# Keys as eight token classes, paired taps in four blocks, gate factors as value columns, and a new written-out order, in a two-layer kernel

## The chip, the cores and the metric

The kernel runs on one core of a Trainium2 chip. The metric is device time in microseconds of one execution. Three runs of the kernel before are at hand, and a profile of one execution, taken by the hardware profiler.

## The reference, cut to what matters

Two layers are computed and written side by side. Layer A is a short filter on the keys, a product with the values, and a convolution over the whole sequence. Layer B is attention in four segments with a memory that is carried from one to the next. S = 2048 tokens, D = 640 channels, H = 32 heads of 20, N = 4 segments of L = 512.

```
def A(q, k, v, shift_k, ssm_k, ssm_D):
    k_shift[t] = sum over j < 4 of k[t - j] * shift_k[:, j]
    kv = k_shift * v
    y = irfft(rfft(kv, 2S) * rfft(ssm_k, 2S))[:S] + kv * ssm_D
    return q * y

def B(x, wq, wk, wv, wo, beta):
    phi = lambda t: where(t > 0, t + 1, exp(t));  g = sigmoid(beta)
    for s in range(4):
        p = softmax(qs @ ks.T * scale + mask)
        a_mem = phi(qs) @ M / (phi(qs) @ z + 1e-6)
        o = g * a_mem + (1 - g) * (p @ vs)
        M = M + phi(ks).T @ vs;  z = z + sum(phi(ks))
    return o @ wo
```

(The mask leaves each query its own place and those before it in the segment.)

## The kernel before, in words

All operations are first recorded by a `Recorder` (line 105 on). A stand-in for the engines takes every call, notes what it reads and writes, and keeps the calls as operations. Two packed tables then say in which order the operations are issued (`ORDER`, line 866) and in which of eight PSUM banks each group of matmuls works (`BASE`, line 889). So the order of each engine's work, and of SyncE's queue, which issues nearly all DMAs and waits in order, is written out by hand or by a search made earlier, and nothing is decided at run time. Since every operation is issued by one helper, all rows of the profile carry its line, L256, and are told apart by their tiles. A third table, `EVICT` (line 863), says for each copy of a PSUM result to SBUF whether ACT (0) or DVE (1) makes it: 31 of 238 are on DVE.

Layer A (`conv`, line 428) goes over five blocks of 128 channels, `dp` 0 to 4.

- `load_filter` (line 437) brings the long filter, turned so that tokens lie on partitions, as `kT`.
- `short_filter` (line 460) brings a block's keys turned by one DMA transpose, channels on partitions, 2048 tokens in a row, as `kr`. There is one such buffer. The filter is applied on PE: the keys of 128 tokens, eight apart, are loaded as weights, and a diagonal matrix of taps (`skd`) is streamed. In blocks 0 and 1 seven matmuls make a group of four token classes, 2048 columns in all. In blocks 2 to 4 (`TAP2`, line 862) the taps are paired: 64 channels and the same 64 shifted by two tokens lie on the two halves of the partitions, and ten matmuls with 1024 columns do the same. For this the keys are copied, shifted, by three DMAs within SBUF: two into a second buffer `kb`, one within `kr`. DVE multiplies the result with the values (`vt`).
- `spectrum` (line 515) multiplies with a table `Wf` and adds and subtracts on DVE, for values (`Xh`) and filter (`Kh`). `product` (line 548) multiplies the two on DVE. `inverse` (line 584) multiplies with `Wi` and with the queries (`pq`).

Layer B goes over eight units `u`, a segment and half of the heads each.

- `project` (line 636) makes keys and queries (`KQ`) and values (`Va`), turns the former (`KQT`) by PE in the first unit and by DMA in the others, and makes phi of keys, all four token tiles at once, and of queries, two tiles at once, each by an exponential on ACT and two operations on DVE. A bound on the scores (`A`, `qabs`, `bT`) goes into `KQT` as a further row. Then the memory is brought forward: 16 matmuls, a product with a block mask (`mt`), a product of one column with a gate factor (`em`), and a sum with the memory so far (`Mbd`).
- `attend` (line 722) fills the scores of four heads (`fill`, line 737), whose exponentials ACT writes to `ET`, 128 x 1024 at a time; `values` (line 775) multiplies them with the values, the memory with the turned phi of queries (`PqT`), takes reciprocals of the sums (`rr`) and scales, on DVE, once for each four heads.
- `project_out` (line 815) multiplies with `wo`; the result goes out by `outb`, at the very end also by the free tile `PP`.

The gate (`beta_setup`, line 396) is carried in column 20 of the values and of the memory, as 1 + e^beta and as e^-beta factors. At the start PE does 20 warm-up matmuls of 512 columns on a tile of zeros (`WARM`, line 854).

Of the kernel before, what the change touches and what calls it, by code (L numbers as in the profile page):

```python
# [21 lines left out]
S = 2048; D = 640  # L22
# [22 lines left out]
def small_consts():  # L45
# [3 lines left out]
    sel = np.zeros((128, 32), np.float32)  # L49
# [4 lines left out]
    for hh in range(4):  # L54
        rows = (hl == hh) & (d < DH)
        maskbd[rows, hh, 0:DH + 1] = 1.0
        epsrow[32 * hh + DH + 1, hh] = EPS
# [207 lines left out]
class Layer:  # L265
    def __init__(self, ctx, tc, A_q, A_k, A_v, A_shift_k, A_ssm_k, A_ssm_D, B_x, B_wq, B_wk, B_wv, B_wo, B_beta, out):
# [14 lines left out]
        self.rings = {}  # L281
# [30 lines left out]
        skr = self.ring("skd", [128, 4, 128])[0:5].rearrange("c a b -> c (a b)")  # L312
# [31 lines left out]
        self.evict(self.taps[:], tp, g)  # L344

# [4 lines left out]
        self.kr = c.tile([128, KPAD + S], bf16, name="kr")  # L350
# [6 lines left out]
        nc.gpsimd.memset(self.kr[:, 0:KPAD], 0.0)  # L357
        self.kb = c.tile([128, KPAD + S], bf16, name="kb")
        nc.gpsimd.memset(self.kb[:, 0:KPAD], 0.0)
# [7 lines left out]
        if WARM:  # L367
            idle = self.ring("o2", [128, 2, 16, DH])[:].rearrange("p a b d -> p (a b d)")
            rec.key = ("warm",)
            nc.vector.memset(idle, 0.0)  # L370
            g = self.group(1, "warm")
            for n in range(WARM):
                rec.key = ("warm", n)
                with rec.one():
                    nc.tensor.matmul(g.ap[:, 0, 0:WARMC], lhsT=idle[:, 0:128], rhs=idle[:, 128:128 + WARMC], start=True, stop=True, grp=g)

# [19 lines left out]
    def beta_setup(self):  # L396
        nc, c, bt = self.nc, self.consts, self.bt
        V = nc.vector
        em = c.tile([128, H], f32, name="em")
# [3 lines left out]
        nc.scalar.activation(out=em[:], in_=g.ap[:, 0, 0:H], func=ACTF.Exp, scale=-1.0, grp=g)  # L403
        ep, ginv = [self.ring("rr", [128, 2, 16], f32, n=2)[:].rearrange("p a b -> p (a b)") for _ in range(2)]
        nc.scalar.activation(out=ep, in_=g.ap[:, 0, 0:H], func=ACTF.Exp, grp=g)
        omginv = c.tile([128, H], f32, name="omginv")
        V.tensor_scalar(out=em[:], in0=em[:], scalar1=1e30, scalar2=None, op0=ALU.min)
        V.tensor_scalar(out=ginv, in0=em[:], scalar1=1.0, scalar2=None, op0=ALU.add)
        V.tensor_scalar(out=omginv[:], in0=ep, scalar1=1.0, scalar2=1e30, op0=ALU.add, op1=ALU.min)
        for h in range(2):  # L410
            V.tensor_copy(out=self.Va[h][:, :, :, DH], in_=omginv[:, None, 16 * h:16 * h + 16].to_broadcast([128, 4, 16]))
        self.emg = em[:].rearrange("p (g h) -> p g h", h=4)
        for h in range(2):
            V.tensor_tensor(out=self.Mbd[h][0][:, :, :, DH], in0=ginv[:, 16 * h:16 * h + 16].rearrange("p (g h) -> p g h", h=4),
                            in1=self.epsrow[:, None, :].to_broadcast([128, 4, 4]), op=ALU.mult)

# [11 lines left out]
    def conv(self, dp):  # L428
# [31 lines left out]
        def short_filter():  # L460
            key("lk")
            kr = self.kr
            if dp in KTURN:
                kn = self.ring("ET", [128, 4, 512], n=ETBUF)[:].rearrange("p (b c) (e d) -> p (b c) e d", c=2, e=4)[:].rearrange("p x e d -> p (x e) d")
                for a in range(2):
                    nc.sync.dma_start(out=kn[:, 8 * a:8 * a + 8], in_=self.k[1024 * a:1024 * a + 1024, dsl].rearrange("(p e) d -> p e d", e=8))
                for x in range(4):
                    key("kn", x)
                    g = self.group(1, "kn")
                    with rec.one():  # L470
                        for e in range(4):
                            nc.tensor.matmul(g.ap[:, 0, 128 * e:128 * e + 128], lhsT=kn[:, 4 * x + e], rhs=self.ident[:], start=True, stop=True, grp=g)
                    at = KPAD + 1024 * (x // 2)
                    self.evict(kr[:, at:at + 1024].rearrange("d (p e) -> d e p", e=8)[:, 4 * (x % 2):4 * (x % 2) + 4], g.ap[:, 0, :].rearrange("d (e p) -> d e p", e=4), g)
            else:
              nc.sync.dma_start_transpose(out=kr[:, KPAD:KPAD + S], in_=self.k[:, dsl])
            if dp in TAP2:
                key("lc")
                q = self.queue("lc", dp)
# [6 lines left out]
            key("skd")  # L486
            skd = self.ring("skd", [128, 4, 128])
            if dp in TAP2:
                skd2 = skd[:].rearrange("p a d -> p (a d)")[:, 0:256].rearrange("p (f l d) -> p f l d", f=2, l=2)
                V.tensor_tensor(out=skd2, in0=self.id2[:, None, None, :].to_broadcast([128, 2, 2, 64]), in1=self.taps[:, 0:4, dp].rearrange("p (f l) -> p f l", f=2)[:, :, :, None].to_broadcast([128, 2, 2, 64]), op=ALU.mult)  # L490
            else:
                V.tensor_tensor(out=skd[:], in0=self.ident[:, None, :].to_broadcast([128, 4, 128]),
                                in1=self.taps[:, 4:8, dp, None].to_broadcast([128, 4, 128]), op=ALU.mult)
            for b in range(4):
                key("ks", b)
                g = self.group(1, "ks")
                ps = g.ap[:, 0, :]
                first = KPAD + 1024 * (b // 2) + 4 * (b % 2)
                if dp in TAP2:
                    with rec.one():  # L500
                        for m in (0, 2, -1, 1, 3):
                            for f, kx in ((0, kr), (1, self.kb)):
                                c0, c1 = max(0, m), min(4, m + 2)
                                nc.tensor.matmul(ps.rearrange("p (c d) -> p c d", d=128)[:, c0:c1, 64 * f:64 * f + 64], lhsT=kx[:, first + m:first + m + 1017:8],
                                                 rhs=skd2[:, f, c0 - m:c1 - m, :], start=(m == 0 and f == 0), stop=(m == 3), grp=g, skip_group_check=True)
                else:
                  with rec.one():
                    for n, dl in enumerate((0, 1, -1, 2, -2, 3, -3)):
                        c0, c1 = max(0, dl), min(4, 4 + dl)
                        nc.tensor.matmul(ps[:, 128 * c0:128 * c1], lhsT=kr[:, first + dl:first + dl + 1017:8], rhs=skd[:, c0 - dl:c1 - dl, :],  # L510
                                         start=(n == 0), stop=(n == 6), grp=g, skip_group_check=True)
                V.tensor_tensor(out=vt[:, b], in0=ps.rearrange("p (c d) -> p c d", d=128), in1=vt[:, b], op=ALU.mult, grp=g)
# [71 lines left out]
        def inverse(U):  # L584
# [3 lines left out]
            for c in range(4):  # L588
                key("I", c)
                g = self.group(1, "I")  # L590
                pyv = g.ap[:, 0, :].rearrange("p (a h d) -> p a h d", a=2, h=2)
# [5 lines left out]
                V.tensor_tensor(out=qd[:, :, c, :], in0=g.ap[:, 0, :].rearrange("p (b d) -> p b d", d=128), in1=qd[:, :, c, :], op=ALU.mult, grp=g)  # L597
# [38 lines left out]
    def project(self, u):  # L636
# [5 lines left out]
        for t in range(4):  # L642
# [14 lines left out]
            self.evict(Va[:, t, :, 0:DH], g.ap[:, 0, 0:320].rearrange("p (h d) -> p h d", d=DH), g)  # L657
# [10 lines left out]
            for i, n in ((0, 4), (1, 2)):  # L668
# [25 lines left out]
        A = self.ring("A", [128, 4, 32], n=1)  # L694
        V.tensor_tensor(out=A[:], in0=self.sel[:, None, :].to_broadcast([128, 4, 32]), in1=kam[:, :, None].to_broadcast([128, 4, 32]), op=ALU.mult)
# [269 lines left out]
```

## Time and profile before

| | |
|---|---|
| median of 3 runs | 273.33 us (272.47 to 273.53) |
| span of the profiled execution | 272.0 us, 10130 instructions |
| busy: PE, weight load, DVE, ACT | 260.8, 195.4, 250.9, 248.8 us |
| mean granted clock of PE | 0.993 |
| DMA | 43.74 MB, mean 161 GB/s |

The profile gives no time of its own execution beside the span. Engines are PE (matmul), PEld (its weight load), DVE, ACT, POOL and SP. A row of a group gives the tiles (result <- operands), the shape, the count, then busy time in us and the mean ns of one, then the idle time of the engine ahead of them and what ended it. A row of the order of time begins with the start and the length in us. A row of a stretch gives its length, busy time and count of PE, PEld, DVE, ACT and POOL, then the granted clock, the DMA engines' share and GB/s. A busy PE is not PE at its peak, since matmuls overlap.

### The profile page before, as it was taken

How to read it: one execution, taken by the hardware profiler on the slowest of the kernel's cores; microseconds unless marked ns; L12 is line 12 of the kernel's file. 1: busy time of each engine (PE TensorE's matmuls, PEld its weight loads, DVE VectorE, ACT ScalarE, POOL GpSimd, SP SyncE). 2: the span in 40 equal slices, each digit the busy share in tenths (PEclk: the TensorE clock that was granted, in tenths of full speed). 3: DMA queues.
4: the chain of work that ended last, by engine and by line, in shares of the span. 5: the costliest groups of instructions: out<-in, count | busy, mean ns of one | idle time of the engine just before them, and what ended most of it. 6: DMA issues, size and time to landing. Idle time of an engine off the chain costs nothing.

```text
span 272.0 us, 10130 instructions
## 1 busy us (share of the span) xinstructions
PE 260.8 (96%) x4368; PEld 195.4 (72%) x4371; DVE 250.9 (92%) x424; ACT 248.8 (91%) x388; POOL 6.9 (3%) x18
## 2 busy tenths in 40 slices
PE   8999999999998999999999999999999989999995
PEld 3879777868766677878676787768677765756783
DVE  0599999999999999999999999999999998999972
ACT  1586799999999999999999999999999998999962
POOL 9100000000000000000000000000000000000000
PEclk9999999999999999999999999999999997999999
DMA  6999399999989599998979599994974081894024
GB/s 166 347 207 243 82 191 225 311 194 172 170 217 201 144 195 195 191 178 159 159 165 190 116 151 226 147 197 65 146 177 82 4 154 27 169 155 90 27 68 133
DMA packets 126972, 43.74 MB, mean 161 GB/s; under 512 B 117339, under 2 KB 124512, under 8 KB 126800
## 3 DMA queue, kind: packets, MB, share of 16 engines
q1 hardware_dynamic: 126768, 42.91, 79.9%
q8 instruction: 34, 0.56, 0.9%
q0 software_dynamic: 160, 0.20, 0.2%
q14 instruction: 10, 0.08, 0.1%
HBM read 14.12 MB, written 7.34 MB: 79 GB/s over the span
## 4 chain that ended last, share of the span: by engine, by line
PE 55%; ACT 33%; issue 6%; DVE 4%; ACTq 0%; DVEq 0%
PE ps L256 55%; ACT ET L256 21%; ACT F L256 4%; ACT KQ L256 3%; ACT PP L256 3%; ACT outb L256 1%; ACT Va L256 1%; DVE F L256 1%; DVE pq L256 1%; DVE Kh L256 1%; ACT bT L256 1%; DVE qabs L256 0%; DVE vt L256 0%; DVE Xh L256 0%; DVE PP L256 0%
## 5 line engine op out<-in xcount | busy, mean ns | idle before, releaser
L256 ACT ACTIVATE ET<-ps 128x1024 bf16<-128x1024 f32 x160 | 160.6, 1102 | 1.9 <-PE ps L256 1.7
L256 PE MATMUL ps<-wqkv,xT 128*128 128x320 bf16 x480 | 76.3, 300 | 0.5 <-ACT ET L256 0.3
L256 PEld LDWEIGHTS <-xT 128*128 128x128 bf16 x640 | 58.1, 98 | 25.7 <-issue 5.2
L256 PE MATMUL ps<-Va,ET 128*128 128x21 bf16 x1280 | 42.4, 172 | 0.3 <-ACT ET L256 0.3
L256 ACT CAST F<-ps 128x512 bf16<-128x512 f32 x69 | 42.0, 687 | 0.3 <-PE ps L256 0.3
L256 PEld LDWEIGHTS <-ET 128*128 128x128 bf16 x1280 | 39.7, 96 | 3.0 <-issue 2.2
L256 PE MATMUL ps<-KQT 32*128 32x128 bf16 (+2 forms) x896 | 34.6, 240 | 1.1 <-ACT ET L256 1.0
L256 PEld LDWEIGHTS <-Wf 128*128 128x128 bf16 x320 | 28.9, 97 | 6.1 <-issue 1.5
L256 ACT CAST KQ<-ps 128x320 bf16<-128x320 f32 x61 | 28.2, 496 | 1.4 <-PE ps L256 1.3
L256 PE MATMUL ps<-wo,xT 128*128 128x320 bf16 x160 | 25.4, 299 | 0.0
L256 PEld LDWEIGHTS <-KQT 32*128 32x128 bf16 x896 | 16.0, 92 | 10.9 <-issue 9.9
L256 PE MATMUL ps<-vt,Wf 128*128 128x256 bf16 x160 | 22.4, 272 | 0.1
L256 PE MATMUL ps<-kT,Wf 128*128 128x256 bf16 x160 | 22.2, 273 | 0.2 <-ACT ET L256 0.2
L256 PE MATMUL ps<-Y,Wi 128*128 128x256 bf16 x160 | 21.7, 280 | 0.0
L256 DVE TENSOR_TENSOR o<-ps,rr 128x640 bf16<-128x640 f32 x24 | 19.5, 814 | 0.2
L256 PE MATMUL ps<-Mbd,PqT 128*128 128x84 bf16 x96 | 18.1, 202 | 1.2 <-ACT ET L256 0.9
L256 DVE TENSOR_TENSOR Y<-Y,pq 128x2048 bf16<-128x2048 bf16 (+1 forms) x20 | 18.6, 945 | 0.0
L256 DVE TENSOR_TENSOR pq<-Xh,Kh 128x2048 bf16<-128x2048 bf16 x15 | 18.1, 1209 | 0.0
L256 PEld LDWEIGHTS <-Wi 128*128 128x128 bf16 x160 | 15.3, 100 | 3.5 <-issue 1.0
L256 ACT ACTIVATE PP<-KQ 128x640 bf16<-128x640 bf16 (+1 forms) x18 | 17.7, 991 | 0.0
L256 PE MATMUL ps<-pack 32*128 32x128 bf16 x512 | 14.7, 216 | 1.9 <-ACT ET L256 1.7
L256 ACT CAST Va<-ps 128x320 bf16<-128x320 f32 x31 | 15.0, 520 | 1.2 <-PE ps L256 1.2
(93 smaller groups left out, 370.0 us busy)
## 6 DMA issues: line engine op xcount, KB each, us to landing
vt<-in_A_v_dram SPq DMA_DIRECT2D x10, 256.0 KB
pq<-in_A_q_dram SPq DMA_DIRECT2D x10, 256.0 KB
out_dram<-outb SPq DMA_DIRECT2D x13, 160.0 KB
turned<-kT SPq DMA_DIRECT2D x4, 512.0 KB
kT<-turned SPq DMA_DIRECT2D x8, 256.0 KB
out_dram<-pq SPq DMA_DIRECT2D x8, 256.0 KB
kb<-kr SPq DMA_DIRECT2D x6, 256.0 KB
Wf<-c_wf SPq DMA_DIRECT2D x4, 256.0 KB
```

Source lines behind the costliest of these rows:

```text
L256: f(*[fix(a) for a in args], **{k: fix(v) for k, v in kw.items()})
```

## The change

- The keys of a block lie in eight classes, one for each token number modulo eight, each with its own padding: eight DMA transposes of 256 tokens in place of one of 2048. The weights of a tap group are then adjacent. The shifted copies take five DMAs in place of three.
- Taps are paired in blocks 1 to 4, no more in 2 to 4 alone. The tap matrices of blocks 0 to 2 are made at the start.
- The gate factors are two columns of the values, 0 and 21, with the 20 channels between them; the dot part uses columns 0 to 20, the memory columns 1 to 21. The product with `em` falls away.
- The memory so far is added in PSUM by a seventeenth matmul with the identity, and one product with the mask writes the new memory.
- Phi of queries is made for four tiles at once, and turned by one DMA.
- In the first segment two groups of four heads share one reciprocal and one scaling.
- The bound's weights have 4 columns in place of 32.
- Ten warm-ups, no longer 20.
- New `EVICT` (38 of 238 on DVE), `ORDER` and `BASE`.

The options `KSW` and `IW` are 1 throughout, so that groups of `ks` and `I` stay as they were; `KTURN` was empty before.

```
-            for i, n in ((0, 4), (1, 2)):
+            for i, n in ((0, 4), (1, 4)):
...
-              nc.sync.dma_start_transpose(out=kr[:, KPAD:KPAD + S], in_=self.k[:, dsl])
+            kv = self.k[:, dsl].rearrange("(P e) d -> e P d", e=8)
+            for e in range(8):
+                nc.sync.dma_start_transpose(out=kr[:, e, KPAD:], in_=kv[e])
             if dp in TAP2:
-                q.dma_start(out=self.kb[64:128, KPAD:KPAD + S], in_=kr[64:128, KPAD:KPAD + S])
-                q.dma_start(out=self.kb[0:64, KPAD:KPAD + S], in_=kr[64:128, KPAD - 2:KPAD + S - 2])
-                q.dma_start(out=kr[64:128, KPAD:KPAD + S], in_=kr[0:64, KPAD - 2:KPAD + S - 2])
+                q.dma_start(out=kb[64:128], in_=kr[64:128])
+                q.dma_start(out=kb[0:64, 2:8], in_=kr[64:128, 0:6])
+                q.dma_start(out=kb[0:64, 0:2, KPAD:], in_=kr[64:128, 6:8, KPAD - 1:-1])
+                q.dma_start(out=kr[64:128, 2:8], in_=kr[0:64, 0:6])
+                q.dma_start(out=kr[64:128, 0:2, KPAD:], in_=kr[0:64, 6:8, KPAD - 1:-1])
+            def tokens(kx, a, e):
+                at = KPAD + 128 * a - (e < 0)
+                return kx[:, e % 8, at:at + 128]
...
-  lhsT=kx[:, first + m:first + m + 1017:8]
+  lhsT=tokens(kx, b // 2, 4 * (b % 2) + m)
...
-        A = self.ring("A", [128, 4, 32], n=1)
+        A = self.ring("A", [128, 4, 4], n=1)
...
-                nc.tensor.matmul(g.ap[32 * k:32 * k + 32, 0, :], lhsT=A[:, k, :], rhs=qabs[:, k, :], start=True, stop=True, grp=g)
+                nc.tensor.matmul(g.ap[32 * k:32 * k + 4, 0, :], lhsT=A[:, k, :], rhs=qabs[:, k, :], start=True, stop=True, grp=g)
...
-                        nc.tensor.matmul(pmv[:, k, :, 0:DH + 1], lhsT=PP[:, 0, t, 4 * k:4 * k + 4, :], rhs=Va[:, t, 4 * k:4 * k + 4, 0:DH + 1],
-                                         start=(t == 0), stop=(t == 3), grp=g)
-            V.tensor_tensor(out=mt[:, :, :, 0:DH + 1], in0=pmv[:, :, :, 0:DH + 1], in1=self.maskbd[:, None, :, 0:DH + 1].to_broadcast([128, 4, 4, DH + 1]), op=ALU.mult, grp=g)
-            V.tensor_tensor(out=mt[:, :, :, DH], in0=mt[:, :, :, DH], in1=self.emg[:, 4 * half:4 * half + 4, :], op=ALU.mult)
-            V.tensor_tensor(out=dst[:, :, :, 0:DH + 1], in0=src[:, :, :, 0:DH + 1], in1=mt[:, :, :, 0:DH + 1], op=ALU.add)
+                        nc.tensor.matmul(pmv[:, k, :, 1:VW], lhsT=PP[:, 0, t, 4 * k:4 * k + 4, :], rhs=Va[:, t, 4 * k:4 * k + 4, 1:VW],
+                                         start=(k == 0 and t == 0), stop=False, grp=g, skip_group_check=True)
+                nc.tensor.matmul(pmv[:, :, :, 1:VW], lhsT=self.ident[:], rhs=src[:, :, :, 1:VW], start=False, stop=True, grp=g, skip_group_check=True)
+            V.tensor_tensor(out=dst[:, :, :, 1:VW], in0=pmv[:, :, :, 1:VW], in1=self.maskbd[:, None, :, 1:VW].to_broadcast([128, 4, 4, DH + 1]), op=ALU.mult, grp=g)
...
+        def values(pp, parts):
+            for j in range(2):
+                if s or not j:
+                    g = self.group(2, "o")
+                weighted(2 * pp + j, *parts[j], g, 0 if s else j)
+                if s == 0 and j == 0:
+                    continue
+                V.reciprocal(out=rr, in_=den, grp=g)
+                if s == 0:
+                    V.tensor_tensor(out=o_s[:, :, h0:h0 + 8, :].rearrange("p q (j h) e -> p j q h e", j=2), ...
+                    continue
...
-WARM, WARMC = 20, 512
+WARM, WARMC = 10, 512
-TAP2 = (2, 3, 4)
+TAP2 = (1, 2, 3, 4)
-ORDER = r"""
-c-jTQ1ArU=3<SVzHo3ZA+qP}nwr$&A+qP}nwr$(iOpwHu2ohIHNIZ!z2_&H;lEjikl1eg3E-56Xh@=uqYDpt$C7q;~@KRn>%1Q>wBjqH&l$LN(QZh;fsV!wBl0Zx
+ORDER = r"""
+c-jrqgO(5q6a~<8E^<w_YqD+Io^0E;ZBMpqvTfV8ZNB#nd+oT0kHkoTBuI*6NRB`hL<*!tDx^jl0L4%og%AmaQ3AOU5k-&|>5v`)h>Q$~jX1~yMI}^0ROE%BBx
```

More of the change, by code (lines that the diff above doesn't have):

```diff
@@ L280, in __init__ @@
         self.real = tc.nc
[L281 removed]
+        self.rings, self.skd = {}, {}
         self.evicts = 0
@@ L344, in __init__ @@
         self.evict(self.taps[:], tp, g)
+        for dp in range(3):
+            self.filter_weights(dp)
         rec.key = ("zero",)
@@ L485, in short_filter @@
             self.halves(self.queue("lv", dp), vt, self.v, dsl)
[L486 to L493, printed above, removed]
+            if dp not in self.skd:
+                self.filter_weights(dp)
+            skd = self.skd[dp]
             for b in range(4):
                 key("ks", b)
-                g = self.group(1, "ks")
-                ps = g.ap[:, 0, :]
-                first = KPAD + 1024 * (b // 2) + 4 * (b % 2)
+                w = KSW[dp]
+                if b % w == 0:
+                    g = self.group(w, "ks")
+                ps = g.ap[:, b % w, :]
                 if dp in TAP2:
@@ L805, in attend @@
+                a, b = [o2[:, i].rearrange("p (q h) e -> p q (h e)", h=4) for i in range(2)]
+                V.tensor_tensor(out=odst[:, :, j], in0=a, in1=b, op=ALU.add)
         for pp in range(2):
```

172 lines of the change are left out of this document (85 added, 87 removed).

## The prediction, as it stood before the run

> **What bounds the kernel now.** I read the clock and span of the core first, then busy time in stretches, then the chain of waits, then groups of instructions with their shapes kept apart, and the order of time at both ends.
>
> ```profile
> core 0: 272.0 us, clock 0.993
> PE 55%; ACT 33%; issue 6%; DVE 4%; ACTq 0%; DVEq 0%
> 10.00:20.00 10.00, 9.95 (x95) 8.14 (x95) 7.99 (x15) 8.60 (x18) 0.00 (x0) 1.00 1.11 253
> 20.00:30.00 10.00, 10.00 (x98) 8.46 (x98) 9.84 (x21) 6.79 (x16) 0.00 (x0) 1.00 0.86 196
> 200.00:210.00 10.00, 10.00 (x211) 7.36 (x211) 10.00 (x21) 10.00 (x17) 0.00 (x0) 1.00 0.49 114
> 260.00:272.00 12.00, 8.58 (x119) 6.49 (x115) 5.68 (x11) 4.43 (x9) 0.00 (x0) 0.99 0.37 110
> ```
>
> The columns after the stretch are its length and the busy time of PE, weight load, DVE, ACT and POOL. From about 40 to 260 us DVE and ACT have no gaps, and the chain passes between PE and ACT. Idle time is in the head, where ACT waits for PE, and in the tail. PE's busy time is no measure of its limit, since it holds overlapped matmuls. So work taken from an engine is worth something where that engine is saturated, and little in head or tail. For ACT the saturated part begins and ends with the first and last exponential (ET):
>
> ```profile
> 33.66 1.98 ACT L256 ACTIVATE ET<-ps 128x1024 bf16<-128x1024 f32 x2
> 259.30 2.03 ACT L256 ACTIVATE ET<-ps 128x1024 bf16<-128x1024 f32 x2
> ```
>
> The last ET ends at 259.30 + 2.03 = 261.33, and 10.7 us follow: last values, projection, stores. The median of the runs, 273.33, is 1.33 above the span of 272.0, and I add that at the end.
>
> **DVE.** The change removes work in four places.
>
> ```profile
> L256 DVE TENSOR_TENSOR mt<-mt,em 128x16 bf16<-128x16 bf16 x6 | 1.3, 212 | 0.0
> L256 DVE TENSOR_TENSOR Mbd<-Mbd,mt 128x336 bf16<-128x336 bf16 x6 | 2.0, 325 | 0.0
> L256 DVE TENSOR_SCALAR qabs<-KQ 128x640 bf16<-128x640 bf16 x12 | 3.7, 308 | 0.0
> L256 DVE TENSOR_SCALAR qabs<-KQ 128x1280 bf16<-128x1280 bf16 x6 | 2.9, 483 | 0.0
> L256 DVE TENSOR_TENSOR PP<-PP,qabs 128x640 bf16<-128x640 bf16 x12 | 5.7, 474 | 0.0
> L256 DVE TENSOR_TENSOR PP<-PP,qabs 128x1280 bf16<-128x1280 bf16 x6 | 4.9, 816 | 0.0
> L256 DVE RECIPROCAL rr<-ps 128x16 f32<-128x16 f32 x8 | 1.8, 240 | 0.2 <-PE ps L256 0.2
> L256 DVE RECIPROCAL rr<-ps 128x32 f32<-128x32 f32 x24 | 8.4, 352 | 1.3 <-ACT ET L256 0.9
> L256 DVE TENSOR_TENSOR o_s<-ps,rr 128x320 bf16<-128x320 f32 x8 | 3.8, 474 | 0.0
> L256 DVE TENSOR_TENSOR o<-ps,rr 128x640 bf16<-128x640 f32 x24 | 19.5, 814 | 0.2
> L256 DVE TENSOR_TENSOR A<-pack,kam 128x128 bf16<-128x128 bf16 x8 | 2.2, 273 | 0.0
> L256 DVE CAST PP<-ps 128x320 bf16<-128x320 f32 x2 | 1.0, 490 | 1.1 <-PE ps L256 1.1
> ```
>
> The memory update loses its second and third operation: 1.3 + 2.0 = 3.3 us. The query side of phi goes from twelve halves to six wholes: 3.7 + 5.7 becomes 2.9 + 4.9, so 1.6 less. In the first segment, eight normalizations become four of double size: 1.8 + 3.8 becomes 4 x (0.352 + 0.814) = 4.7, so 0.9 less. The bound's A shrinks from 128 to 16 elements, and the nearest row of that size is 212 ns, so 8 x 0.06 = 0.5. That is 6.3 us. Against it the new table puts 38 evictions on DVE instead of 31. But five of the seven come behind the last attention result, where DVE had gaps, so two remain, 2 x 0.49 = 1.0. DVE's work ahead of its tail falls by about 5.3 us. The beta set-up (one operation for three) and the filter weights, made earlier, I cost at nothing, since they are issued in the head, where DVE waits for PE; without that cover they are a few tenths either way. One thing could be dearer: in the first segment the two banks of a pair are now freed together, so the first is held until the second head group is summed. I take nothing for it, because six banks are left, and 0.8 us at most, one normalization.
>
> **ACT.** It gains least, and so it decides.
>
> ```profile
> L256 ACT ACTIVATE PP<-KQ 128x640 bf16<-128x640 bf16 x12 | 9.8, 815 | 0.0
> L256 ACT ACTIVATE PP<-KQ 128x1280 bf16<-128x1280 bf16 x6 | 8.1, 1343 | 0.0
> L256 ACT CAST KQ<-ps 128x320 bf16<-128x320 f32 x61 | 28.2, 496 | 1.4 <-PE ps L256 1.3
> ```
>
> Phi saves 9.8 - 8.1 = 1.7. Seven evictions leave ACT, but behind the last ET there were seven and now stands one, so six of them leave the tail. Ahead of the last ET only one goes, 28.2 / 61 = 0.46. The term is 1.7 + 0.5 = 2.2 us.
>
> **The head.** On ACT the first ET moves ahead of five other evictions. ACT before, the stretch to the first ET (F is spectrum, KQT turned keys, Va values):
>
> ```order
> L256 CAST bT_113<-ps 128x512
> L256 CAST Va_84<-ps 128x16x20 x2
> L256 CAST KQT_86<-ps 128x4x128
> L256 CAST KQ<-ps 128x16x20
> L256 CAST Va_84<-ps 128x16x20
> L256 ACTIVATE ET_120<-ps 128x1024 x2
> ```
>
> ACT of the changed kernel, the same stretch:
>
> ```order
> L257 CAST bT_118<-ps 128x512
> L257 CAST KQT_95<-ps 128x4x128 x2
> L257 CAST Va_93<-ps 128x16x20
> L257 CAST KQT_95<-ps 128x4x128
> L257 CAST KQ<-ps 128x16x20 x2
> L257 ACTIVATE ET_78<-ps 128x1024
> ```
>
> Two values projections now stand behind the first ET. What PE need no longer do before it:
>
> ```profile
> 5.07 0.15 PEld L256 LDWEIGHTS <-o 128*128 128x128 bf16 x1 [0.28 <-issue]
> 5.50 1.42 PEld L256 LDWEIGHTS <-o 128*128 128x128 bf16 x7 [0.28 <-issue]
> 7.04 0.73 PEld L256 LDWEIGHTS <-kT 128*128 128x128 bf16 x8
> 15.66 4.24 PE L256 MATMUL ps<-wqkv,xT 128*128 128x320 bf16 x30
> 19.95 3.49 PE L256 MATMUL ps<-skd,kr 128*128 128x384 bf16 x27
> ```
>
> The first warm-ups stand 0.43 apart (5.07 to 5.50), the later ones 1.42 / 7 = 0.2; the ten dropped are late ones, 2.1 us. Two projections are 10 x 4.24 / 30 = 1.4, one tap group of block 1 (now behind the first ET) 3.49 / 4 = 0.9. One more turning of keys takes back 0.2. PE reaches the first ET 4.2 us earlier, at 29.5, if its data are there. Some 0.9 us of ACT's evictions are moved behind it, so at most 3.3 us of ACT's idle time go. At least nothing goes: the DMA share of 1.11 between 10 and 20 us says that loads may be what comes late once PE is early. I take 1.4, nearer the middle than the full amount because of that row.
>
> **The taps.** Two rows price the class layout:
>
> ```profile
> L256 PEld LDWEIGHTS <-kr 128*128 128x128 bf16 x116 | 14.4, 149 | 1.7 <-issue 0.2
> L256 PEld LDWEIGHTS <-Wf 128*128 128x128 bf16 x320 | 28.9, 97 | 6.1 <-issue 1.5
> 71.55 0.22 PE L256 MATMUL ps<-skd,kr 128*128 128x128 bf16 x1
> 72.08 0.23 PE L256 MATMUL ps<-skd,kb 128*128 128x64 bf16 x1
> ```
>
> Weights read at every eighth token load in 149 ns, adjacent ones in 97. A paired group of ten matmuls starts its last one 0.53 us after its first, about 0.59 us whole. If it becomes bound by its columns (half of a plain group's, so 0.87 / 2 = 0.44), three blocks gain 12 x 0.15 = 1.8, and block 1, newly paired, 4 x (0.87 - 0.44) = 1.7. [...] Neither is in my sum, since PE follows ACT there; what the change adds on PE, one matmul of 336 columns in each of six memory sums at the pace of a 320-column projection, 4.24 / 30, is 0.8 us and covered in the same way. The bound's matmuls stream the same 512 columns into fewer rows and stay as they are; query transposes go from twelve to six of double size, the same blocks.
>
> **The tail.** All eight last evictions now go to DVE: 8 x 0.49 = 3.9 us, beside 29 matmuls at 0.14 = 4.1 us. So 0 to 0.5 later; I take 0.3.
>
> **The sum.** 261.3 - 2.2 - 1.4 = 257.7 for the last ET, + 10.7 + 0.3 = 268.7 of span, + 1.33 = 270.0. DVE's 5.3 us and PE's relief are worth nothing by themselves: ACT's 2.2 is the smallest of the three, so ACT is late next. I take the new order to be as dense as the old, whose body leaves DVE and ACT no gap to gain or lose in most stretches. With the head's full 3.3 and no tail cost it is 267.8; with nothing from the head and 0.5 in the tail 271.6.
>
> **Rivals.**
>
> *Slower: block 1's keys come late.* SyncE's queue in the changed kernel, keys of block 1, has (kr turned by class, kb the shifted copy, bT the bound's rows):
>
> ```order
> L257 DMA KQT_95<-bT_118 4x512 x2
> L257 DMA wqkv<-in_B_wv_dram 128x5x320
> L257 DMA_TRANSPOSE kr<-in_A_k_dram 128x256 x2
> L257 DMA vt_112<-in_A_v_dram 128x8x128
> L257 DMA KQT_95<-bT_118 4x512
> L257 DMA kb<-kr 64x2176
> L257 DMA kb<-kr 64x1632
> L257 DMA kb<-kr 64x2x256
> L257 DMA vt_112<-in_A_v_dram 128x8x128
> L257 DMA kr<-kr 64x2x256
> L257 DMA kr<-kr 64x1632
> ```
>
> Where one transpose stood, there are now eight, with five copies behind them, and each in-order wait holds all that follows: the turned filter, block 1's values, the next keys.
>
> ```profile
> 29.21 0.69 SPq L256 DMA_DIRECT2D KQT<-bT  x1
> 9.84 5.53 SPq L256 DMA_TRANSPOSE kr<-in_A_k_dram  x1
> 23.88 2.45 SPq L256 DMA_TRANSPOSE kr<-in_A_k_dram  x1
> 55.00 1.62 SPq L256 DMA_DIRECT2D kb<-kr  x2
> 62.32 0.50 SPq L256 DMA_DIRECT2D kr<-kr  x1
> pack<-c_pack POOLq DMA_DIRECT2D x1, 184.0 KB, 7.2
> Drow<-in_A_ssm_D_dram POOLq DMA_DIRECT2D x1, 1.2 KB, 4.0
> ```
>
> A piece costs 0.31 to 0.69 us (an eighth of 2.45 or 5.53). The bound's rows, at 29.21 before, come about 2.1 earlier with PE, so 27.1. From there two rows 1.4, a weight 0.6, two pieces 0.6 to 1.4, vt and a row 1.3, three kb copies 2.4: 33.4 to 34.2. The kr copies overwrite what kb's copies read, and must wait for their landing; landings shown are 4.0 to 7.2 us, and theirs before took under 5.7 (56.62 to 62.32). Then 1.0 to issue and a second landing: 42.4 with 4.0 each, 46 with 5.7. PE reaches these taps after its first ET and 50 more projections, 50 x 4.24 / 30 = 7.1, so at 36.6, and with the score blocks and memory sum between them, for which I allow 2 us, at 38.6. That is a stall of 4 to 7 us. ACT has some scores in PSUM to work on when the stall begins. It makes the kernel slower only if over 4.7 us come through to ACT (270.0 to 274.7): then up to 277. For it speaks that PE works in order, so all scores behind these taps wait with them. Against it: both landings are of loads from DRAM, and copies within SBUF may land sooner; and it can happen once, since blocks 2 to 4 have the same chain with tens of us ahead of them.
>
> *No change: the head stays as it was and the order packs worse.* The gain is then ACT's 2.2, and 2 us of new gaps, which the 220 us of saturated body can hold, take it back: 272.0 to 274.7.
>
> *Ten warm-ups are too few.* The pace changed at 5.50 here, and ten warm-ups at 0.43 last 4.3 us, so they end where the change came, with none to spare. If it comes later, the two rows of kT's weights (0.73 for eight, twice) and the first spectrum matmuls double: up to 2 us, which is the head's whole gain of 1.4 and a little: about 271.5. [...]
>
> *Faster:* the full head, and no second loss of the clock.
>
> ```profile
> 220.00:230.00 10.00, 8.67 (x159) 6.05 (x157) 8.70 (x15) 8.66 (x11) 0.00 (x0) 0.83 0.46 82
> ```
>
> Here the clock was 0.83, and DVE and ACT lost 1.3 us each. 267.8 - 1.3 = 266.5.
>
> **How the numbers follow.** Forecast 0.50 (267.8 to 271.6), faster rival 0.13, too few warm-ups 0.06, no change 0.16, late keys 0.15. A measurement here tells about 0.5% from no change, 1.4 us. Faster by over that (below 271.96): 0.50 + 0.13 + 0.06 = 0.69; within it 0.16; slower 0.15. The range leaves out the slower case and the far end of the faster one: 266.3 to 274.7.
>
> **What would show it.** Right: last ET ends near 257.7; the first near 31; ACT's busy time 243 to 245 and DVE's 247 to 249; tap weights near 100 ns; kT's weights load before 7.04. Wrong: a wait of PE on the taps of block 1 near 40 us; kT matmuls 0.1 us apart; gaps on ACT between 45 and 255 us; a tail over 11.2 us after the last ET.

## The result, and the profile after

| | before | after |
|---|---|---|
| median | 273.03 us (272.47 to 273.53, 4 runs) | 306.92 us (306.43 to 309.82, 4 runs) |
| ratio | | 1.127, 95% interval 1.122 to 1.132 |
| span of the profiled execution, mean clock | 272.0 us, 0.993 | 305.3 us, 0.955 |
| first ET begins, last ET ends | 33.66, 261.33 us | 38.37, 294.12 us |
| from the last ET to the end | 10.7 us | 11.2 us |

Medians are of all executions of a kernel; ratios and intervals leave out single executions that were clearly slower than its others, among them one of block1_single at 799.76 us, which nothing here explains.

The change makes the kernel slower by 33.9 us, and nearly all of it lies ahead of the last exponential. The chain of waits of the changed kernel says of what kind the loss is (before: PE 55%, ACT 33%, and no DMA or queue at all; SPq is SyncE's queue):

```profile
PE 30%; ACT 24%; DMA 20%; SPq 12%; DVE 9%; issue 5%; ACTq 0%; DVEq 0%
```

So some 32% of 305 us, about 98 us of the path, is now transfers and the queue that issues them. Busy time in stretches shows where the engines starve (columns as in the prediction; the last is 90 us long):

```profile
30.00:40.00 10.00, 6.47 (x63) 3.99 (x64) 9.72 (x11) 4.89 (x10) 0.00 (x0) 0.83 0.60 151
80.00:110.00 30.00, 23.96 (x383) 16.62 (x382) 23.59 (x33) 22.41 (x35) 0.00 (x0) 0.83 0.59 122
110.00:140.00 30.00, 25.52 (x444) 19.10 (x442) 21.97 (x33) 24.51 (x35) 0.00 (x0) 0.94 1.03 205
210.00:300.00 90.00, 86.15 (x1625) 62.95 (x1622) 86.59 (x140) 82.89 (x118) 0.00 (x0) 0.98 0.58 111
```

Until the keys of the last block have come (their last piece is issued at 188.5), PE, DVE and ACT have gaps in most stretches; from 140 to 180, where each is busy for 38 of the 40 us, they have few. From 80 to 110 it isn't that the DMA engines are full: their share is 0.59 there, and the kernel before had more in the same stretch:

```profile
80.00:110.00 30.00, 28.99 (x473) 21.41 (x471) 29.72 (x49) 30.00 (x49) 0.00 (x0) 1.00 0.91 190
```

From 110 to 140 the share is 1.03, with gaps all the same. From 210 on the kernel is about as dense as before. In some of the stretches with gaps the granted clock is lower too (0.83 from 30 to 40 and from 80 to 110). The waits of the changed kernel name many transfers, no single one (total, times, longest):

```profile
PE ps L257 <- DMA KQT<-bT: 5.5, 3, 3.4
PE ps L257 <- DMA wo<-in_B_wo_dram: 4.4, 1, 4.4
PE ps L257 <- DMA kr<-kr: 3.9, 2, 2.5
PE ps L257 <- DMA wqkv<-in_B_wv_dram: 3.1, 1, 3.1
ACT KQ L257 <- DMA KQT<-KQ: 2.9, 1, 2.9
```

What these have in common is SyncE, which issues them in order. SyncE in order of time, the head (rows of other tiles left out; the last row is of the kernel before):

```profile
9.05 8.57 SPq L257 DMA_TRANSPOSE kr<-in_A_k_dram  x6
24.59 3.74 SPq L257 DMA_TRANSPOSE kr<-in_A_k_dram  x3
28.38 0.57 SPq L257 DMA_DIRECT2D wqkv<-in_B_wv_dram  x1
29.00 5.25 SPq L257 DMA_TRANSPOSE kr<-in_A_k_dram  x3
34.97 1.31 SPq L257 DMA_DIRECT2D KQT<-bT  x2
36.86 2.57 SPq L257 DMA_TRANSPOSE kr<-in_A_k_dram  x2
41.26 1.94 SPq L257 DMA_DIRECT2D kb<-kr  x3
...
16.76 1.48 SPq L256 DMA_DIRECT2D wqkv<-in_B_wv_dram  x1
```

Six pieces of 256 tokens hold the queue for 8.57 us. Value weights, bound's rows, shifted keys stand behind pieces; before, the value weights were issued at 16.76 and the rows at 29.21, now at 28.38 and 34.97. The tile's own view gives the price (minimum, median and maximum in ns), first of the changed kernel, then of the kernel before:

```profile
L257 SPq DMA_TRANSPOSE kr<-in_A_k_dram x40: 1102/1240/2675, 7.0 to 188.5; - x40
L256 SPq DMA_TRANSPOSE kr<-in_A_k_dram x5: 2193/3418/5529, 9.8 to 124.0; - x5
L256 SPq DMA_TRANSPOSE KQT<-KQ x28: 1234/1340/4917, 37.1 to 221.8; - x28
```

A piece, two squares of 128 x 128, costs 1.24 us of SyncE, and so do the eight squares of a KQT transpose (1.34). Added up over all rows of the order of time, short waits inside a row with them, SyncE was occupied for 201 of 272 us before, and for 246 of 305 after; the forty pieces are 55.7 us of it, where five whole turns were 17.4. (The expectations below have 236 us for 246, and 199 for a run that has 202; they were summed without some rows.)

### The profile page after: what moved, and what is told of

Its sections match the earlier page's. It is cut to its first block, busy times and chain, and to the rows that moved or that the text cites. A ratio compares the mean times of both kernels' runs of the same rounds, so it can differ in the third digit from the quotient of the medians.

```text
span 305.3 us, 10161 instructions
## 1 busy us (share of the span) xinstructions
PE 268.3 (88%) x4379; PEld 195.4 (64%) x4379; DVE 254.0 (83%) x397; ACT 248.1 (81%) x375; POOL 7.0 (2%) x18
## 3 DMA queue, kind: packets, MB, share of 16 engines
q1 hardware_dynamic: 129088, 43.86, 70.5%
## 4 chain that ended last, share of the span: by engine, by line
PE 30%; ACT 24%; DMA 20%; SPq 12%; DVE 9%; issue 5%; ACTq 0%; DVEq 0%
PE ps L257 30%; ACT ET L257 13%; SPq L257 12%; ACT F L257 4%; DMA kb<-kr 2%; DMA out_dram<-outb 2%; DMA xT<-in_B_x_dram 2%; ACT KQ L257 2%; DMA Wf<-c_wf 2%; DMA wo<-in_B_wo_dram 2%; DMA kr<-kr 2%; ACT PP L257 2%; DMA wqkv<-in_B_wv_dram 2%; DVE pq L257 1%; ACT outb L257 1%
## 5 line engine op out<-in xcount | busy, mean ns | idle before, releaser
L257 ACT ACTIVATE ET<-ps 128x1024 bf16<-128x1024 f32 x160 | 162.3, 1110 | 12.1 <-PE ps L257 11.9
L257 PEld LDWEIGHTS <-xT 128*128 128x128 bf16 x640 | 60.0, 100 | 41.0 <-issue 15.9
L257 PE MATMUL ps<-wqkv,xT 128*128 128x320 bf16 x480 | 79.3, 309 | 7.3 <-DMA wqkv<-in_B_wv_dram 3.1
L257 PEld LDWEIGHTS <-ET 128*128 128x128 bf16 (+1 forms) x1292 | 39.7, 97 | 6.0 <-issue 4.3
L257 ACT CAST F<-ps 128x512 bf16<-128x512 f32 x71 | 40.8, 642 | 1.6 <-PE ps L257 1.2
L257 PE MATMUL ps<-KQT 32*128 32x128 bf16 (+2 forms) x896 | 35.8, 247 | 6.0 <-DMA KQT<-bT 5.5
L257 ACT CAST KQ<-ps 128x320 bf16<-128x320 f32 x58 | 26.8, 490 | 8.1 <-PE ps L257 5.0
L257 PEld LDWEIGHTS <-KQT 32*128 32x128 bf16 x896 | 16.9, 94 | 16.8 <-issue 15.7
L257 DVE TENSOR_TENSOR pq<-ps,pq 128x512 bf16<-128x512 f32 x20 | 13.6, 685 | 7.6 <-PE ps L257 5.5
L257 DVE TENSOR_TENSOR vt<-ps,vt 128x512 bf16<-128x512 f32 x20 | 13.0, 685 | 8.2 <-PE ps L257 5.3
L257 DVE RECIPROCAL rr<-ps 128x32 f32<-128x32 f32 x28 | 9.9, 352 | 8.0 <-ACT ET L257 7.5
## 6 DMA issues: line engine op xcount, KB each, us to landing
kb<-kr SPq DMA_DIRECT2D x4, 272.0 KB
```

The lines of the kernel that those rows point to most:

```text
L257: f(*[fix(a) for a in args], **{k: fix(v) for k, v in kw.items()})
```

## The experiments

My theory after reading the trace was the number of transposes (theory 1 in the first runs). The rivals: the new written-out order packs worse (2), the five shifted copies take the time (3), source rows eight tokens apart are slow to fetch (4). Where operations go or come, the rest keep the order that the named kernel has, and a new one stands at the first place where its inputs are there.

| run | what it is | median us | ratio to before, 95% |
|---|---|---|---|
| classes_one_turn | changed kernel, one transpose per block into the classes | 287.44 | 1.0468 to 1.0542 |
| one_turn | changed kernel, keys laid out as before | 285.2 | 1.032 to 1.0463 |
| before_8_pieces | before, its transpose cut in eight | 304.6 | 1.1063 to 1.1177 |
| before_compute | before, with the arithmetic edits | 277.16 | 1.0143 to 1.0187 |
| one_turn_loads | one_turn, four loads moved ahead | 279.43 | 1.0143 to 1.0284 |
| after_resorted | changed kernel, SyncE's queue in another order | 296.68 | 1.0754 to 1.0873 |
| one_turn_resorted | one_turn, SyncE's queue in another order | 274.75 | 1.0028 to 1.0079 |
| before_resorted | before, SyncE's queue in another order | 275.66 | 1.0036 to 1.0107 |
| one_turn_all | one_turn_resorted, all engines moved a little | 281.59 | 1.0278 to 1.0348 |
| extra_turns | one_turn_resorted and 35 idle transposes | 288.3 | 1.0509 to 1.057 |
| block1_single | one_turn_resorted, block 1 not paired | 275.24 | 1.0055 to 1.0101 |
| before_compute_phi2 | before_compute, phi of queries by two tiles | 275.03 | 1.0026 to 1.0072 |

### The number of transposes

```
-            for e in range(8):
-                nc.sync.dma_start_transpose(out=kr[:, e, KPAD:], in_=kv[e])
+            nc.sync.dma_start_transpose(out=kr[:, :, KPAD:], in_=self.k.rearrange("(P e) d -> P (e d)", e=8)[:, 128 * dp:128 * dp + 1024])
```

> The changed kernel with one transpose per channel block in place of eight: it fills the same eight rows of kr with the same number of bytes from source rows as far apart, five instructions instead of forty, but takes the first 1,024 numbers of every eighth row, so the keys are not the right ones. Order, contiguous weights and the five shifted copies stay as in the changed kernel. Theory 1 (each transpose holds SyncE's queue for some 1.1 us however small it is, 40 of them some 51 us): 35 instructions go, about 35 us of SyncE, the waits on DMA go, and the time falls to 266 to 273 us. Theory 2 (the new order of operations packs worse): stays at 295 to 307. Theory 3 (the five shifted copies and the rows that they touch): stays above 290. Theory 4 (source rows 8 tokens apart are slow to fetch): each single transpose takes 8 us or more and the time stays above 290.

Measured 287.44 us: 19.5 us of the 33.9 go with the 35 instructions, with the bytes, the source step, the weights' layout and the five copies all left in place. That is about half of the 34 to 41 us that theory 1 expected, and not all of it: 287 stays well above 273. SyncE's tile view:

```profile
L257 SPq DMA_TRANSPOSE kr<-in_A_k_dram x5: 2110/2389/5437, 7.1 to 137.4; - x5
```

Sixteen squares from rows as far apart as in the pieces take 2.11 us and more, as in the kernel before (2.19). The pieces tell the same: 1,240 ns in the median here, from rows eight apart, and 1,242 in a run further down (before_8_pieces), from neighbouring rows. So theory 4 falls: here rows eight apart do not hold SyncE longer.

The second run goes back to the layout of before altogether (`kr` a row of tokens, `lhsT=kx[:, at:at + 1017:8]`, one transpose, three copies):

> The changed kernel with the layout of keys of the kernel before: kr a single row of tokens, one transpose, three shifted copies, weights read with a step of 8; all the rest (pairs in four blocks, gate columns, memory in PSUM, ten warm-ups, the new order) as changed. Theory 1 (number of transposes): 267 to 275 us, with tap weights at 149 ns again. Theory 2 (the order): 295 or more. Theory 3 (five copies): 267 to 275 too, since the copies are three again; it is told apart by the run with eight rows and one transpose. Theory 4 (source step): 267 to 275.

285.2 us. Against the run before it this differs by 2.2 us, about what the two intervals leave open; so the two extra copies cost little (theory 3), and the adjacent weights, which this run gives up, gave nothing that shows, unless the two offset each other. Some 12 us remain with the new order and the other edits.

The third turns the question round and spoils the kernel before:

```
-              nc.sync.dma_start_transpose(out=kr[:, KPAD:KPAD + S], in_=self.k[:, dsl])
+              for e in range(0, S, 256):
+                  nc.sync.dma_start_transpose(out=kr[:, KPAD + e:KPAD + e + 256], in_=self.k[e:e + 256, dsl])
```

> The kernel before with its one transpose of 2,048 tokens per block cut into eight of 256 neighbouring tokens, issued one behind the other, into the same single row; nothing else changed. Theory 1: 35 more instructions at 1.0 to 1.2 us on SyncE; with its queue fuller by some 34 us the time grows to 290 to 308 us if all of it is on the path, at least 280 if half is hidden. Theories 2 and 3: 272 to 275, since order and copies are those of before. Theory 4 (source rows 8 tokens apart): 272 to 275, since these rows are neighbours; each piece then takes 0.3 us.

304.6 us, 31.3 more than before, by one edit. SyncE in order of time at block 1, then the tile's view and the chain of waits of the same run:

```profile
30.98 10.94 SPq L256 DMA_TRANSPOSE kr<-in_A_k_dram  x8
42.03 0.68 SPq L256 DMA_DIRECT2D KQT<-bT  x1
```

```profile
L256 SPq DMA_TRANSPOSE kr<-in_A_k_dram x40: 1165/1242/3295, 9.2 to 157.3; - x40
```

```profile
PE 39%; ACT 19%; SPq 15%; DMA 12%; DVE 7%; issue 6%; ACTq 0%; DVEq 0%
```

Eight neighbouring pieces take 10.94 us where one transpose took 2.45, and the bound's rows behind them come at 42.03 instead of 29.21. In an order that was made for one transpose of 2.45 us, the pieces cost more than in the changed one, which spreads them out.

### What stands behind what in SyncE's queue

> The run with the layout of before and the rest as changed (285.2 us), and four loads that wait for nothing moved ahead in SyncE's queue, to where the order of before has them: the value weights and the second query weights of the projections and the second super-tile's x ahead of the transposes of block 1, and the output weights behind Wi. Theory 2a (what is left of the loss is the place of free loads behind transposes that wait): the wait for the output weights (7.5 us plus 2 of queue in the chain) and that for the value weights (4.0 us) go and the time is 271 to 278 us. Theory 2b (the loss is spread over the order of the arithmetic): 282 to 287 us.

In one_turn the value weights were issued at 26.30, behind a transpose that waited for block 0's taps (24.22), and the output weights at 109.77, 7.7 us ahead of their use. SyncE of one_turn in order of time:

```profile
24.22 2.03 SPq L257 DMA_TRANSPOSE kr<-in_A_k_dram  x1
26.30 0.58 SPq L257 DMA_DIRECT2D wqkv<-in_B_wv_dram  x1
...
109.77 0.44 SPq L257 DMA_DIRECT2D wo<-in_B_wo_dram  x1
```

And PE of one_turn, with what it waited for in brackets:

```profile
117.44 1.49 PE L257 MATMUL ps<-wo,xT 128*128 128x320 bf16 x5 [3.16 <-DMA wo<-in_B_wo_dram]
```

With four loads moved the time is 279.43, 5.8 less: short of the 271 to 278 of theory 2a, below the 282 to 287 of 2b. Free loads behind waiting ones are part of the loss. So the whole queue was put in another order, found by a search over SyncE's instructions alone, for the changed kernel, for one_turn and, as a control, for the kernel before.

> The changed kernel with its forty transposes, every instruction of PE, ACT, DVE and POOL in the changed kernel's order; only SyncE's queue stands in another order, in which an instruction that can go at once does not stand behind one that waits, and a piece of a transpose stands behind what is needed sooner (value weights and second super-tile ahead of block 1's keys, output weights some 40 instructions earlier). Theory A (forty transposes fill the queue, 236 us of work in 305, whatever their order): 293 to 307 us. Theory B (236 us of queue fit into 270, and the loss is in what stands behind what): 268 to 280 us.

> The same with the layout of before (one transpose per block, strided weights; 285.2 us in the changed order, 279.4 with four loads moved): SyncE's queue in another order, the other engines' as in the changed kernel. Theory B: the waits on DMA go almost wholly and the arithmetic's saving shows, 264 to 271 us, below the kernel before. Theory C (the new order of the arithmetic or the edits themselves lose the last 6.4 us): 276 to 280 us.

> Control: the kernel before with SyncE's queue put in another order in the same way, nothing else changed. Its engines wait for no DMA in the chain now, so both theories expect 270 to 275 us; below 268 would mean that the sorting itself is worth what the other two runs gain.

Together with the runs in the changed order these make a square:

| | 40 transposes | 5 transposes | difference |
|---|---|---|---|
| queue as changed | 306.92 | 285.2 | 21.7 |
| queue in the other order | 296.68 | 274.75 | 21.9 |
| difference | 10.2 | 10.5 | |

The two causes add: about 22 us for the number of transposes, in either order, and about 10 us for the order of SyncE's queue. By the intervals each difference is known to 2 or 3 us only; the other order is one for each kernel, found for it; and the kernel with 5 transposes has the layout and the copies of before with them. 296.68 lies in theory A's range, but not for its reason alone: the order is worth 10 us. The control came out at 275.66, 0.4 to 1.1% above before, so that kind of reordering is no gain by itself. one_turn_resorted is 1.7 us above before (273.01 in the runs beside it), not below it: theory B's 264 to 271 did not come, nor theory C's 276 to 280.

> The layout of before with SyncE's queue sorted as in the run before, and small moves among the instructions of PE, ACT, DVE and POOL too. Theory B: 263 to 271 us, not more than 1 us from the run with only SyncE sorted, since the engines' own order is not what loses the time. Theory C: over 2 us below that run.

281.59, 6.8 us above the run with SyncE's order alone. Neither theory said that; the moves among the engines were bad ones, and the run tells nothing about the cause.

### Queue or chain

Why do forty transposes still cost 22 us in a better order? In the chain of waits of after_resorted, block 1's keys stand as a run, pieces, rows, copies, landing, shifted copies, landing:

```profile
34.33 1.12 SPq L257
35.50 1.24 SPq L257
...
40.66 3.76 DMA kb<-kr
...
46.34 3.65 DMA kr<-kr
```

`kr` is one buffer, so pieces can start only when the block before has read its keys, and all eight must be issued ahead of the copies (the rows shown begin with two of block 1's pieces and end with the second landing). Is it this chain that loses the time, or the fuller queue? To one_turn_resorted 35 transposes were added that take part in no chain:

```
+        for i in range(35):
+            nc.sync.dma_start_transpose(out=junk[i % 2][:], in_=self.k[128 * (i % 16):128 * (i % 16) + 128, 0:128])
```

> The run with SyncE's queue sorted and one transpose per block (274.75 us), and 35 more transposes of 128 tokens spread evenly over SyncE's queue; they wait for nothing and nothing reads what they write. Theory A1 (the number of transposes fills the queue): 35 times 1.1 us or more, 38 us more of a queue that was occupied for 199 of 274 us, and 290 to 300 us. Theory A2 (the queue has room, and the forty lose by the chain of eight in a row between the last tap of a block and the copies of the next): 275 to 281 us.

288.3 us: 13.6 more, between the two. The tile view of this run, and its chain of waits, which had DMA 10% and SPq 2% without them:

```profile
L257 SPq DMA_TRANSPOSE junk<-in_A_k_dram x35: 1110/1235/1845, 26.8 to 265.9; - x35
```

```profile
PE 37%; ACT 20%; DMA 16%; DVE 13%; SPq 7%; issue 6%; DVEq 0%; ACTq 0%
```

Each costs 13.6 / 35 = 0.39 us of the kernel's time, a third of its 1.24 on the queue, though nothing reads what it writes. So of the 22 us about 14 are the fuller queue (the 35 also move 1.15 MB, which this run doesn't separate from issuing them). The other 8 would fit the chain of eight pieces ahead of the copies, of which the chain of waits above holds the last two; that part was not taken away by itself (a second buffer for `kr` would do it), and it stays an inference.

### The rest: arithmetic and pairing

> The kernel before, in its own order and with its own keys (one transpose, three blocks with paired taps, twenty warm-ups, single quarters of super-tile 0), with only these edits of the change: phi of the queries over four tiles (one 16-block transpose in place of two of 8), the gate factors as value columns, memory's sum in PSUM, the four-column bound weights. Theory 2 (the arithmetic pays and the new order loses it): 267 to 271 us, since ACT loses 1.7 us and DVE 5 us and the order that waits on nothing from DMA stays. Rival (the arithmetic doesn't pay or itself makes the waits, as the one late transpose of phi behind four tiles): 274 to 285 us.

277.16 us, 4.2 slower. The arithmetic does not pay in the order of before. The chain of waits of this run at one place, the turned queries:

```profile
204.06 4.50 PE ps L257 x124
208.57 4.69 DMA PqT<-PP
213.34 1.27 ACT PP L257
```

With phi over four tiles one transpose of 16 squares is issued where the last of two stood, and the units behind it wait for the landing.

> The kernel before with the gate columns, memory's sum in PSUM and the four-column bound weights, in its own order, but with phi of the queries over two tiles as before. With phi over four tiles the same kernel took 277.16 us. Theory P (phi over four tiles makes the transposed queries late, 4.7 us of DMA behind a transpose of 16 blocks in the chain): 271 to 273.5 us. Theory M (memory's matmul, which must now wait for the gate's columns and holds phi of the keys behind it, 2.3 us of ACT between 40 and 60 us): 274.5 to 277 us.

275.03, so phi over four tiles was half of the 4.2 us by the medians, and some two thirds by the middle of the intervals (1.65% falls to 0.49%). The rest stayed, in theory M's range. The trace shows a gap at M's place: phi of the keys on ACT, and what ACT waited for ahead of it, in this run and then in the kernel before:

```profile
43.62 1.02 ACT L257 ACTIVATE ET<-ps 128x1024 bf16<-128x1024 f32 x1 [0.43 <-PE ps L257]
46.02 1.27 ACT L257 ACTIVATE PP<-KQ 128x1280 bf16<-128x1280 bf16 x1 [1.38 <-PE ps L257]
...
42.15 1.31 ACT L256 ACTIVATE PP<-KQ 128x1280 bf16<-128x1280 bf16 x1
```

Those are 1.8 us of ACT's time. That the gate's columns, for which memory's matmul waits, bring them was not tried by itself.

> The run with SyncE's queue sorted and one transpose per block (274.75 us), with block 1's taps one at a time as in the kernel before: its three shifted copies go, its filter weights take a tile of their own. Theory D (the chain of transpose, copies and shifted rows, 4.36 and 4.70 us in the chain between 34 and 44 us, delays block 1 and idles ACT for 2.1 us between 40 and 60): 271 to 273.5 us, though PE has 1.7 us more to do. Rival (the copies are hidden there): 274.5 to 276.5 us.

275.24 against 274.75, no difference: the rival holds. The copies do go from the chain of waits, and nothing is won by it:

```profile
PE 48%; ACT 30%; DVE 13%; issue 4%; DMA 3%; SPq 1%; ACTq 0%; DVEq 0%
```

## Why the prediction was wrong, point by point

**The step that failed** is the price of a piece. It stood in the rival on late keys: "A piece costs 0.31 to 0.69 us (an eighth of 2.45 or 5.53)". It took a part's time as the same part of the whole's. At that price forty pieces are 12 to 28 us of SyncE, beside the 17 of before, and the queue seems to gain little. Measured, a piece costs 1.10 at least and 1.24 in the median, two to four times that, and the forty took 55.7 us. The trace of before had a row that comes near it: the smallest transpose there, a KQT of half the size, took 1.234 us and more, and nothing in the trace was a transpose at less. At that row's 1.23 the forty come to 49 us of SyncE, 32 more than the 17 of before.

**What the sum left out** is SyncE's queue. I read from the chain, which had no SyncE in it, that the queue was free. It was occupied for 201 of 272 us, but in an order that let nothing in the chain wait for it. The sum has a term for ACT, one for DVE and one for PE, and none for the queue to which the change added 35 instructions; the eight pieces were priced at one place, block 1. The runs put about 22 of the 33.9 us on the number of transposes.

**The rival on late keys** had the mechanism and the first place right. Block 1's taps were reached at 49.25, after kb's copies had landed in 3.54 us and kr's in 3.16, both sooner than the 4.0 to 5.7 that I allowed. But the chain began later than the 27.1 that it starts from: the bound's rows were issued at 34.97, since six of block 1's pieces stood ahead of them, 9.0 us (3.74 and 5.25) instead of the 1.9 to 4.1 that six cost at the predicted price. PE in order of time:

```profile
49.25 0.23 PE L257 MATMUL ps<-skd,kr 128*128 128x128 bf16 x1 [1.42 <-DMA kr<-kr]
```

But it was priced at up to 277 because it "can happen once, since blocks 2 to 4 have the same chain with tens of us ahead of them". They have not: the engines have gaps in most stretches until 210. Its chance of 0.15 was the one for "slower", and the range ended 32 us below the result.

**"I take the new order to be as dense as the old"** is the second step that failed. It is not. With the transposes taken back, one_turn is 12 us slower than before, and 10 of these go when SyncE alone is sorted anew. A price list in the kernel's `Recorder` gives a transpose on its queue by its bytes alone (`op.dur = 5.1 * size / 1024`, 0.33 us for a piece). That the search for the order went wrong by this price would fit, and was not tried.

**The terms on the engines** came out about as reckoned, one by one, and no gain shows of them. Groups of the changed kernel, by shape:

```profile
L257 DVE TENSOR_TENSOR Mbd<-ps,pack 128x336 bf16<-128x336 f32 x6 | 3.0, 503 | 5.8 <-PE ps L257 5.8
L257 DVE TENSOR_TENSOR A<-pack,kam 128x16 bf16<-128x16 bf16 x8 | 1.3, 164 | 0.1
L257 ACT ACTIVATE PP<-KQ 128x1280 bf16<-128x1280 bf16 x12 | 16.2, 1350 | 0.1
L257 PEld LDWEIGHTS <-kr 128*128 128x128 bf16 x108 | 9.8, 100 | 8.4 <-issue 3.3 <-DMA kr<-in_A_k_dram 2.0 <-DMA kr<-kr 1.8
```

Memory's update is one operation of 503 ns, A takes 164 ns (212 was my bound), phi's exponentials 16.2 us for 17.9. In the best arrangement, one_turn_resorted, they should show, since no engine waits there for any one transfer longer than 1.4 us, though DMA and SPq are still 12% of its chain. ACT of that run, the first and the last ET in order of time, and then the group of all:

```profile
33.08 1.02 ACT L257 ACTIVATE ET<-ps 128x1024 bf16<-128x1024 f32 x1
...
260.66 1.94 ACT L257 ACTIVATE ET<-ps 128x1024 bf16<-128x1024 f32 x2 [0.27 <-PE ps L257]
```

```profile
L257 ACT ACTIVATE ET<-ps 128x1024 bf16<-128x1024 f32 x160 | 164.0, 1118 | 2.5 <-PE ps L257 2.4
```

The first begins at 33.08 (33.66 before: 0.6 gained in the head, 1.4 forecast) and the last ends at 262.60 (261.33). The body between takes 1.9 us more, not 2.2 less. Busy time from the first ET's begin to the last one's end, before and then in one_turn_resorted:

```profile
33.66:261.33 227.67, 221.29 (x4002) 166.31 (x4002) 222.64 (x374) 225.47 (x341) 0.00 (x0) 0.99 0.83 156
33.08:262.60 229.52, 222.77 (x4030) 167.33 (x4029) 223.88 (x343) 225.85 (x337) 0.00 (x0) 1.00 0.87 160
```

ACT has four instructions fewer there, but 0.4 us more of busy time, and its gaps grow from 2.2 to 3.7 us. So ACT's 2.2 us, on which the sum rested, didn't come even with the queue in order. The group of the exponentials, which the change doesn't touch, was 160.6 and 1102 before, and is busy 3.4 us longer, more than phi's 1.7. Of that 2.6 us is the mean of one, 1118 for 1102 ns, and 0.8 is less overlap (160 means exceed the busy time by 14.9 us, for 15.7 before); why, no run shows. In the order of before (before_compute_phi2) the edits without phi over four tiles made the kernel 2 us slower too. Why two orders both end at 275 is open. The test that I named, busy time of 247 to 249 on DVE, was no test: DVE was busy for 253.2 us in one_turn_resorted, for 250.9 before, though its groups add up to some 3.5 us less.

**The taps.** Adjacent weights loaded in 100 ns in the changed kernel, as the row said, against 149 at a step of eight before. That is 188 loads x 0.05 = 9 us of weight load, and classes_one_turn, which has five copies for three, was no faster than one_turn for it; the prediction had the taps at nothing in its sum. The runs that differ in the layout show the same: 147 ns in the median at a step of eight (one_turn), 98 without (classes_one_turn).

**Ten warm-ups** were enough in the changed kernel: kT's weights began at 5.07, its 16 turning matmuls took 1.41 us, and the granted clock was 1.00 up to 30 us. In the profiled execution of one_turn_resorted, with ten too, the clock was lower for a while:

```profile
10.00:12.00 2.00, 2.00 (x20) 1.31 (x19) 0.65 (x2) 0.00 (x0) 0.00 (x0) 0.50 1.26 337
8.87 1.89 PE L257 MATMUL ps<-kT,Wf 128*128 128x256 bf16 x8 [0.64 <-DMA Wf<-c_wf]
```

PE had waited there for loads, 0.72 us at 5.6 and 0.64 at 8.2, the clock was 0.50 from 10 to 12, and eight matmuls that take 1.04 us in the changed kernel took 1.89. So the doubling that the rival on warm-ups priced did come there (1.89 for 1.04), and a part of the head's missing gain in that run is of this kind; whether the ten warm-ups or the waits for loads brought it, no run shows. **The tail** took 11.2 us, 0.5 more, for 0.3 forecast.

## What to carry to other kernels

Price the part of a DMA transpose that is cut up by the smallest such instruction in the trace, not by the same part of the whole; where the trace has none as small, by the whole of the smallest (here 1.23 us at the least for eight squares, and 1.24 in the median for a piece of two). An in-order queue that doesn't appear in the chain of waits is not a free one: add up what it issues, set that beside the span, and give it a line in the sum like any engine, since here, with SyncE occupied for 202 of 274 us, each transpose more cost 0.39 us even where nothing read what it wrote. And an order that is written out is made for its own instructions: change their prices, and the place of every load in the queue is to be looked at again.

## What the runs showed of the hardware

- At the least, the time that a DMA transpose holds SyncE grew far less than its size: 1.11 us for one square of 128 x 128 (extra_turns), 1.10 for two and 1.23 for the eight of a KQT (changed kernel), 1.26 once for the sixteen of `kr` (one_turn_resorted) and 2.02 to 2.19 for them in one_turn, classes_one_turn and before. Longer ones came too, up to 6.7 us in one_turn_resorted; what held them no run shows by itself. Plain DMAs took about half of a piece's 1.24 us: 0.56 (KQT<-bT), 0.60 (kb<-kr) and 0.53 (kr<-kr) in the median before.
- Source rows eight tokens apart held SyncE no longer than neighbouring ones (at the least 2,110 ns in classes_one_turn and 2,193 before for 16 squares; 1,240 in the changed kernel and 1,242 in before_8_pieces in the median for two).
- The DMA engines worked as long in the slow kernel as in the fast one, 70.5% of 305.3 us and 79.9% of 272.0, that is 215 and 217 us: the moving took no more time, while SyncE's rows grew from 201 to 246 us. The rows (packets, MB, share), before and changed:

```profile
q1 hardware_dynamic: 126768, 42.91, 79.9%
q1 hardware_dynamic: 129088, 43.86, 70.5%
```
